# Warming matmuls back in front and all engine orders replaced, in a one-core linear attention with a squared-ReLU layer pair

## The chip, the cores and the metric

The kernel runs on one core of a Trainium2 chip. The metric is device microseconds of one execution. Five instruction streams work side by side and meet at semaphores: PE (matmuls), DVE (VectorE), ACT (ScalarE), POOL (GpSimd) and SP, which here only issues DMAs. POOL issues DMAs as well as computing.

## The reference

```python
# q, k, v, alpha: (4 batches, 8 heads, 768 tokens, 48), fp32
for t in range(S):
    state = alpha[:, :, t, :, None] * state + einsum('bhd,bhe->bhde', k[:, :, t], v[:, :, t])
    y[:, :, t] = einsum('bhd,bhde->bhe', q[:, :, t], state)
x = y.transpose(0, 2, 1, 3).reshape(3072, 384)
h = maximum(x @ w_in, 0)          # w_in (384, 2048)
out = (h * h) @ w_out             # w_out (2048, 384)
```

A recurrence over tokens with a decay per channel, then two dense layers with a squared ReLU between them.

## The kernel before

**Units.** The tokens are cut into 12 units of 256 tokens (three per batch, the batches taking turns). Each unit goes through a front (decays), scores, an output, a first dense layer and a second one. A number behind an underscore is the unit: `ln3` is the logarithm of unit 3.

**One unit.** Four loads bring alpha, k, q and v (`lda`, `ldk`, `ldq`, `ldv`) into RAW. ACT takes the Ln of alpha (`ln`), PE sums it over tokens with a triangular matrix (`m1`, `m1i`, `m1s`), ACT takes Exp of the sums with both signs (`ei`, `ea`, `es`) and of the total (`ec`). DVE multiplies k and q with them into QKS (`ekm`, `eqm`, lines 597, 731, 736). From unit 2 on, a product of the two alphas of a pair of tokens comes first (`pr`, lines 658 and 660) and `bk`, `aq` multiply one alpha back in (lines 687 to 698). QKS is transposed into KQT, for units 0 to 2 by PE with copies out (`tr`, `et`), from unit 3 on by two DMA transposes on SP (`tr0`, `tr1`, line 747). PE makes the scores (`p`, line 925) into two PSUM banks, DVE masks them (`mk`, line 936). `kv` makes the unit's own state, `sa`, `sc`, `sd` carry the state on, `y` is the attention output. It is copied (`xe`), transposed (`xt`; from unit 4 on by a DMA on SP) and, in the first units, copied once more (`xv`). `vc` casts v.

**The dense layers.** `s1_g_u` are eight blocks of six matmuls with 256 columns (line 1029); each ends in a relu out of PSUM (`re`, ACT line 1037 or DVE line 1039), and the relus are squared into GT (`sq`, DVE line 1047, POOL line 1050, ACT line 1051), two blocks at a time for the first six, one at a time for the last two. The relu's PSUM banks are mostly two halves used in turn. `s2_g_j_n` are blocks of four matmuls with 384 columns (line 1070) that read GT; `oe` copies their sum out, `out` stores it. The weights come in five pieces (`win0` to `win2`, `wout0`, `wout1`), loaded by POOL.

**What sets the order.** `ORDERS` holds, for every engine, the full list of its operations by name; which list a name stands in decides which engine does it, for those that have alternatives. `schedule()` walks these lists with a table of costs to get a planned start for each operation, and `place()` derives from the operations' reads and writes which semaphore waits are needed. No engine reorders anything: an operation that waits holds up all behind it in its list. Loads are gated besides (`AFTER`, `BEHIND`): win0 and the loads of k and alpha of unit 1 wait for alpha of unit 0 to land, win1 and q, v of unit 1 for k of unit 0, win2 for q of unit 0, unit 2's for win1, unit 3's for wout0, and each later unit's alpha for the q of the unit before.

**Warming matmuls.** `fill()` puts matmuls of ZERO by ZERO into the gaps of PE's planned start, from the landing of the memset of ZERO (an operation that is named `#19`) up to the first `s1_` block. In the lists of before, `#19` is DVE's last operation, behind everything else, so no such matmul is made.

**Named by number.** `#1` to `#13` and `#16` to `#18` are memsets on DVE; `#14`, `#15`, `#20` to `#22` are mask selects on POOL (`#21`, `#22` the two causal masks), `#23` is ACT's copy of half of a causal mask, `table` the load of ACT's function table.

The lines that place the warming matmuls:

```python
    pr.schedule()
    pr.fill(lambda n: lambda pe: pe.matmul(psO[:, 0:n], ZERO[:, 0:128], ZERO[:, 0:n], skip_group_check=True),
            ((512, 216, 420), (256, 109, 250)), min(o.start for o in pr.order["pe"] if o.name.startswith("s1_")), zero, 4600)
    pr.place()
```

and those of the load of a unit:

```python
            ring, cost, at = "sp", 600, L_PRIO[g] + j
            if name in QUEUE:
                ring, cost, at = "pool", 930, -6e5 + QUEUE.index(name)
            load_op[name] = add(ring, lambda e, dst=dst, src=src: e.dma_start(dst, src), cost, at,
                writes=[key], name=f"ld{name}", dma=f"{nm}{r}{ring}", lag=1230 if ring == "sp" else 1180, ...)
```

Of the kernel before, what the change touches and what calls it, by code (L numbers as in the profile page):

```python
# [3 lines left out]
ALU = mybir.AluOpType  # L4
# [9 lines left out]
        table ln0_0 ln1_0 ei0_0 #23 ei1_0 ea0_0 ec0_0 ea1_0 vc0 et01_0 ec1_0 ln1 ei1 ea1 xe0 et0_1 ec1 re0_2 re0_0  # L14
        re0_1 sq0_3 re0_5 re0_4 ln2 re0_6 re0_7 es2 ei2 sq0_7 re1_2 ea2 re1_3 sq0_6 re1_5 et1_2 re1_6 sq1_7 sq1_6
        sq1_5 ec2 sq1_1 ln3 oe0_0 ei3 ea3 ec3 es3 vc3 oe1_0 lm4 ln4 ei4 ea4 ec4 oe0_1 es4 re2_0 re2_1 oe1_1 re2_3
        sq2_3 re2_4 ln5 lm5 ei5 ea5 ec5 xe3 re2_7 re2_6 sq2_6 es5 re3_0 re3_1 oe2_0 vc5 re3_3 lm6 xe4 ln6 re3_4 ei6
        oe2_1 re3_7 ea6 ec6 es6 oe3_0 re4_1 re4_0 re4_3 ln7 xe5 ei7 ea7 lm7 ec7 es7 sq4_5 re4_6 re4_7 re5_0 re5_1
        sq4_7 sq4_6 re5_2 ln8 xe6 oe4_0 ei8 ea8 lm8 re5_5 re5_4 es8 sq5_5 re5_6 re5_7 re6_0 re6_1 sq5_6 ln9 re6_3 lm9
        re6_4 re6_5 ei9 ea9 es9 re6_7 re6_6 sq6_7 oe5_1 re7_1 re7_0 vc9 ln10 sq7_3 re7_5 ei10 lm10 ea10 re7_7 es10  # L20
        sq7_7 oe6_1 re8_1 sq7_5 re8_0 sq7_6 ln11 xe9 lm11 ei11 re8_4 oe7_0 re8_6 re8_5 sq8_6 ea11 re8_7 sq8_1 re9_0
        oe7_1 re9_2 es11 sq8_7 re9_4 oe8_0 xe10 sq9_1 re9_5 oe8_1 sq9_5 sq9_6 re10_1 oe9_0 oe9_1 re10_4 re10_5 re10_6
        re10_7 oe10_0 oe10_1 re11_4 sq11_5 re11_7 oe11_0 oe11_10
    """,
    "dve": """
        #7 #11 #4 #6 #5 #9 #10 #16 #12 #8 #13 #3 #1 #17 ekm0_0 ekm1_0 eqm0_0 #18 eqm1_0 et00_0 et10_0 et11_0 sa0 mk0_0
        mk1_0 ekm1 eqm1 xv0 et1_1 sc0 mk1_1 mk0_1 sa1 #2 re0_3 sq0_1 xe1 pr2 xv1 sq0_5 sc1 re1_0 re1_1 bk2 ekm2 eqm2
        re1_4 et0_2 re1_7 mk1_2 mk0_2 sa2 pr3 sc2 bk3 eqm1_3 ekm3 aq3 eqm0_3 pr4 xe2 sa3 xv2 lb4 ekm4 eqm1_4 eqm0_4
        sc3 re2_2 mk1_3 mk0_3 re2_5 sq2_5 sa4 ekm5 xv3 sc4 lb5 eqm1_5 eqm0_5 mk1_4 mk0_4 re3_2 sq3_3 sa5 re3_5 sc5
        sq3_5 bk6 ekm6 re3_6 lb6 eqm1_6 eqm0_6 mk1_5 mk0_5 re4_2 sq4_1 sa6 re4_4 re4_5 sc6 lb7 oe3_1 ekm7 eqm1_7  # L30
        eqm0_7 mk1_6 mk0_6 sd6 re5_3 sa7 sc7 sq5_3 lb8 ekm8 oe4_1 eqm1_8 eqm0_8 mk1_7 mk0_7 sq5_7 sq6_1 re6_2 xe7
# [25 lines left out]
        #22 #15 #21 #14 #20 lda1 ldk1 ldq1 win1 win0 ldv1 win2 lda2 ldq2 ldk2 ldv2 vc1 wout0 wout1 aq2 sq1_3 sd1 sd0
        vc2 sd2 bk4 sq2_1 pr5 vc4 sd3 bk5 sq2_7 sq3_1 sd4 pr6 sq3_7 sq3_6 vc6 sd5 pr7 sq4_3 bk7 vc7 pr8 sq5_1 bk8 vc8
        pr9 sq6_3 bk9 sq6_6 sq6_5 vc10 bk11 vc11 sq9_3 sq9_7 sq10_1 sq10_6 sq11_1 sq11_3
    """,  # L60
    "sp": """
        lda0 ldk0 ldq0 ldv0 lda3 ldq3 ldk3 ldv3 lda4 ldk4 ldv4 ldq4 tr0_3 tr1_3 lda5 ldk5 tr0_4 tr1_4 out0_1 ldq5 ldv5
        out1_1 lda6 tr0_5 ldk6 tr1_5 ldq6 xt4 ldv6 lda7 tr0_6 ldk7 tr1_6 ldq7 xt5 ldv7 out2_1 lda8 tr0_7 ldk8 tr1_7
        ldq8 xt6 ldv8 out3_1 lda9 tr0_8 ldk9 tr1_8 ldq9 xt7 ldv9 lda10 out4_1 tr0_9 tr1_9 ldk10 ldq10 ldv10 xt8 lda11
        out5_1 ldk11 out6_1 tr1_10 tr0_10 xt9 ldq11 ldv11 out7_1 tr0_11 tr1_11 xt10 out8_1 xt11 out9_1 out10_1 out11_0
        out11_10 out11_11
# [25 lines left out]
class Program:  # L92
# [65 lines left out]
    def schedule(self):  # L158
# [17 lines left out]
        shared = {"dve": 0.0, "pool": 0.0}  # L176
# [17 lines left out]
        while True:  # L194
# [167 lines left out]
def bass_gla_recurrent__then__act_relu_squared_kernel(  # L362
# [27 lines left out]
    RATIO = 4  # L390
    NRAW, NQKS, NKQT, NPM, NV, NXT, NGT, NRR, NOSB = 4, 3, 3, 2, 4, 4, 2, 4, 2
# [111 lines left out]
    def weight(name):  # L503
# [9 lines left out]
        load_op[name] = add("pool", lambda e: e.dma_start(dst, src), 930, -6e5 + QUEUE.index(name), writes=[(key, w)], name=name,  # L513
# [4 lines left out]
    def hd(ap):  # L518
        return ap.rearrange("p (h d) -> p h d", h=H)
# [9 lines left out]
    def load(g):  # L529
# [7 lines left out]
        for j, t, nm in ((0, alpha, "a"), (1, k, "k"), (2, q, "q"), (3, v, "v")):  # L537
# [5 lines left out]
            if name in QUEUE:  # L543
                ring, cost, at = "pool", 930, -6e5 + QUEUE.index(name)
            load_op[name] = add(ring, lambda e, dst=dst, src=src: e.dma_start(dst, src), cost, at,
                writes=[key], name=f"ld{name}", dma=f"{nm}{r}{ring}", lag=1230 if ring == "sp" else 1180,
# [106 lines left out]
    def decays_by_pair(g, p0, r, la, last):  # L653

        def al(j):
            return RAW[r][:, 0, :, j, :]
# [3 lines left out]
            alts={"pool": (lambda e: e.tensor_tensor(hd(PRD[la][:]), al(0), al(1), ALU.mult), pool_ns(HD))})  # L660
# [26 lines left out]
        add("pool", lambda e: e.tensor_tensor(hd(EK[la][:, 0, :]), hd(EK[la][:, 1, :]), al(1), ALU.mult), pool_ns(HD),  # L687
# [3 lines left out]
        if g < RATIO:  # L691
# [4 lines left out]
            add("pool", lambda e: e.tensor_tensor(hd(EQ[la][:, 0, :]), hd(EQ[la][:, 0, :]), al(0), ALU.mult), pool_ns(HD),  # L696
# [462 lines left out]
```

## Time and profile before

| | us |
|---|---|
| median of 3 runs | 176.27 |
| the runs | 173.71, 176.27, 177.86 |
| the profiled execution | 173.93 |
| its span, first to last instruction | 172.2 |
| PE busy / DVE / ACT / POOL | 160.9 / 117.2 / 104.5 / 64.6 |

The page of the profile gives the busy time of each engine, then the span in 40 slices with a digit for tenths of busy time, then the chain of work that ended last. The chain in order of time lists start, length, engine, tile and line of each piece. The timeline lists start, length, engine, line, operation, output and inputs, and in brackets the idle time before it with what ended it. Rows of grouped instructions end in busy time, mean nanoseconds of one, and idle time before them. A row of the table of stages begins with the stretch and its length, and gives busy time and count for each engine.

### The profile page before, as it was taken

How to read it: one execution, taken by the hardware profiler on the slowest of the kernel's cores; microseconds unless marked ns; L12 is line 12 of the kernel's file. 1: busy time of each engine (PE TensorE's matmuls, PEld its weight loads, DVE VectorE, ACT ScalarE, POOL GpSimd, SP SyncE). 2: the span in 40 equal slices, each digit the busy share in tenths (PEclk: the TensorE clock that was granted, in tenths of full speed). 3: DMA queues.
4: the chain of work that ended last, by engine and by line, in shares of the span. 5: the costliest groups of instructions: out<-in, count | busy, mean ns of one | idle time of the engine just before them, and what ended most of it. 6: DMA issues, size and time to landing. Idle time of an engine off the chain costs nothing.

```text
span 172.2 us, 5038 instructions
## 1 busy us (share of the span) xinstructions
PE 160.9 (93%) x2200; PEld 127.6 (74%) x2200; DVE 117.2 (68%) x186; ACT 104.5 (61%) x190; POOL 64.6 (37%) x65
## 2 busy tenths in 40 slices
PE   0696999999999999999999999999999999999994
PEld 0564799756788877887877887878777877687773
DVE  4478889768977787769566848799517709355241
ACT  2837478767677866466785578377668454152240
POOL 4947214910286554481640466001012122403700
PEclk9999999999999999999999999999999999999999
DMA  5999999999997999999999999999983672220012
GB/s 139 346 256 244 291 276 212 204 272 297 159 240 183 292 221 179 221 222 251 205 221 293 219 197 243 162 286 317 183 209 115 90 84 93 48 93 0 24 71 91
DMA packets 71559, 33.37 MB, mean 194 GB/s; under 512 B 67568, under 2 KB 68592, under 8 KB 71536
## 3 DMA queue, kind: packets, MB, share of 16 engines
q1 hardware_dynamic: 69024, 26.75, 70.4%
q0 software_dynamic: 2512, 6.29, 15.4%
q8 instruction: 17, 0.28, 0.7%
q14 instruction: 6, 0.05, 0.1%
HBM read 25.17 MB, written 4.72 MB: 174 GB/s over the span
## 4 chain that ended last, share of the span: by engine, by line
PE 90%; DVE 3%; ACT 2%; DMA 2%; issue 1%; DVEq 0%; ACTq 0%
PE psWH L1029 36%; PE psO L1070 33%; PE psX L925 3%; PE psZ L796 2%; PE psX L828 2%; DMA raw<-in_alpha_dram 2%; PE psX L817 2%; PE psWH L1070 2%; PE psX L997 2%; PE psZ L925 1%; PE psWH L669 1%; DVE pm L936 1%; PE psO L1029 1%; PE psX L864 1%; PE psX L971 1%
## 5 line engine op out<-in xcount | busy, mean ns | idle before, releaser
L1029 PE MATMUL psWH<-xt,win 128*128 128x256 bf16 x552 | 71.0, 274 | 0.2 <-ACT rr L1037 0.2
L1070 PE MATMUL psO<-wout,gt 128*128 128x384 bf16 x352 | 66.3, 326 | 0.0
L1029 PEld LDWEIGHTS psWH<-xt,win 128*128 128x128 bf16 x552 | 61.4, 129 | 5.3 <-DVE xt L983 0.6
L1070 PEld LDWEIGHTS psO<-wout,gt 128*128 128x128 bf16 x352 | 33.4, 98 | 17.5 <-DVE gt L1047 0.5
L1037 ACT ACTIVATE rr<-psWH 128x512 bf16<-128x512 f32 x58 | 33.9, 595 | 15.4 <-PE psWH L1029 14.5
L1050 POOL TENSOR_TENSOR gt<-rr 128x1024 bf16<-128x1024 bf16 (+1 forms) x17 | 28.0, 1654 | 37.4 <-ACT rr L1037 20.8
L1039 DVE TENSOR_SCALAR rr<-psWH 128x512 bf16<-128x512 f32 x34 | 23.4, 690 | 19.5 <-PE psWH L1029 19.0
L1051 ACT ACTIVATE gt<-rr 128x512 bf16<-128x512 bf16 (+1 forms) x26 | 21.1, 824 | 5.8 <-DVE rr L1039 5.8
L1077 ACT ACTIVATE osb<-psO 128x384 f32<-128x384 f32 x18 | 8.8, 490 | 17.0 <-PE psO L1070 16.8
L936 DVE TENSOR_TENSOR pm<-psZ,caus 128x1024 bf16<-128x1024 f32 x12 | 14.6, 1220 | 3.1 <-PE psZ L925 3.1
L726 POOL CAST vbf<-raw 128x768 bf16<-128x768 f32 x8 | 6.7, 832 | 24.6 <-DMA raw<-in_v_dram 24.6
L936 DVE TENSOR_TENSOR pm<-psX,caus 128x1024 bf16<-128x1024 f32 x12 | 14.6, 1216 | 0.5 <-PE psZ L925 0.5
L1047 DVE TENSOR_TENSOR gt<-rr 128x1024 bf16<-128x1024 bf16 (+1 forms) x17 | 10.6, 625 | 2.9 <-ACT rr L1037 2.4
L687 POOL TENSOR_TENSOR ek<-ek,raw 128x384 f32<-128x384 f32 x6 | 6.5, 1082 | 15.8 <-ACT ek L680 15.8
L731 DVE TENSOR_TENSOR qks<-raw,eq 128x384 bf16<-128x384 f32 x18 | 9.4, 553 | 2.6 <-DMA raw<-in_q_dram 1.8
L736 DVE TENSOR_TENSOR qks<-raw,ek 128x768 bf16<-128x768 f32 x11 | 10.5, 955 | 0.5 <-POOL ek L687 0.4
L704 DVE TENSOR_TENSOR la<-psWH,la 128x384 f32<-128x384 f32 x8 | 4.4, 553 | 7.9 <-ACT eq L682 6.5
L661 ACT ACTIVATE lab<-prd 128x384 bf16<-128x384 f32 x10 | 5.2, 522 | 4.1 <-POOL prd L660 2.4
L956 ACT ACTIVATE xbf<-psX 128x768 bf16<-128x768 f32 x7 | 5.7, 810 | 3.3 <-PE psX L817 3.0
L660 POOL TENSOR_TENSOR prd<-raw 128x384 f32<-128x384 f32 x5 | 5.2, 1040 | 4.9 <-DMA raw<-in_alpha_dram 4.9
L680 ACT ACTIVATE ek<-psWH 128x384 f32<-128x384 f32 x10 | 4.9, 490 | 3.0 <-PE psWH L672 2.2
L958 DVE CAST xbf<-psX 128x768 bf16<-128x768 f32 x5 | 4.8, 954 | 2.0 <-PE psX L817 1.3
(128 smaller groups left out, 183.7 us busy)
## 6 DMA issues: line engine op xcount, KB each, us to landing
out_dram<-osb SPq DMA_DIRECT2D x11, 384.0 KB, 4.0
raw<-in_alpha_dram SPq DMA_DIRECT2D x10, 384.0 KB, 4.5
raw<-in_k_dram SPq DMA_DIRECT2D x10, 384.0 KB, 4.6
raw<-in_q_dram SPq DMA_DIRECT2D x10, 384.0 KB, 4.8
raw<-in_v_dram SPq DMA_DIRECT2D x10, 384.0 KB, 4.9
wout<-in_moe_w_out_dram POOLq DMA_DIRECT2D x2, 768.0 KB, 8.4
raw<-in_alpha_dram POOLq DMA_DIRECT2D x2, 384.0 KB, 6.5
raw<-in_k_dram POOLq DMA_DIRECT2D x2, 384.0 KB, 7.2
```

What stands on the lines that cost most here:

```text
L731: add("dve", lambda e, j=j, dst=dst: e.tensor_tensor(dst, RAW[r][:, 2, :, j, :].rearrange("p (n x) d -> p n x d", x=2), EQ[la][:, j].rearr ...
L736: add("dve", lambda e, a=a, E=E: e.tensor_tensor(QKS[qs][:, a, :, :, 0:D], RAW[r][:, 1 + a].rearrange("p h j d -> p j h d"), E[la][:].rear ...
L925: ins = pe.matmul(psT[64 * c:64 * c + 64, rr_, o:o + 128], keys, mov)
L936: add("dve", lambda e, hf=hf, psT=psT: e.tensor_tensor(PM[pm][:, hf].rearrange("p r n j t -> p (r n) (j t)"), psT[:, :, :].rearrange("p r ...
L1029: ins = pe.matmul(psF[:, i * T:(i + 1) * T], WIN[:, kk, hidden(fj)], mov, start=(kk == 0), stop=(kk == KT - 1))
L1037: add("act", lambda e, psF=psF, rr=rr: e.activation(rr, psF, AF.Relu), act_ns(512), pu + 600, reads=[keyF], writes=[("rr", rb, half)], nam ...
L1039: alts={"dve": (lambda e, psF=psF, rr=rr: e.tensor_scalar(rr, psF, 0.0, None, ALU.max), dve_ns(512))})
L1047: add("dve", lambda e, dst=dst, sq=sq: e.tensor_tensor(dst, sq, sq, ALU.mult), 148 + k * 267, pu + 1200, reads=[("rr", rb, h) for h in ran ...
L1050: alts={"pool": (lambda e, dst=dst, sq=sq: e.tensor_tensor(dst, sq, sq, ALU.mult), 200 + k * 840), "act": (lambda e, dst=dst, sq=sq: e.act ...
L1051: "act": (lambda e, dst=dst, sq=sq: e.activation(dst, sq, AF.Square), act_ns(k * 512))})
L1070: ins = pe.matmul(psS, GT[gt][:, fj, j, :], WOUT[:, fj, :], start=(fj == 0), stop=(fj == FT - 1))
L1077: add("act", lambda e, j=j, psS=psS: e.activation(OSB[ob][:, j], psS, AF.Copy), act_ns(DM), ps_ + 700, reads=[keyS], writes=[("osb", ob, j ...
```

## The change

All five lists of `ORDERS` are new. 121 operations change their engine: 36 from DVE to ACT, 34 from ACT to DVE, 18 from POOL to DVE, 14 from ACT to POOL, 12 from DVE to POOL and 7 from POOL to ACT among the computing ones, beside one load. On PE the same blocks stand in another order. The planner's costs change, which act on the placing of the warming matmuls and on the lists that are written out, not on what an operation does. Loads of units 1 to 3 may stand in SP's or POOL's list; the lists put alpha of unit 1 (`lda1`) on SP and leave the others where they were.

The beginnings of the lists, and the stretches of PE's list around the scores of unit 6 and of SP's around its transposes:

```diff
  "act":
-  table ln0_0 ln1_0 ei0_0 #23 ei1_0 ea0_0 ec0_0 ea1_0 vc0 et01_0 ec1_0 ln1 ei1 ea1 xe0 et0_1 ec1 re0_2 re0_0
+  table #23 ln0_0 ln1_0 ei0_0 ea0_0 ei1_0 ea1_0 ec0_0 ec1_0 et00_0 ln1 ei1 ea1 xe0 et0_1 xv0 ec1 re0_1 re0_0
  "dve":
-  #7 #11 #4 #6 #5 #9 #10 #16 #12 #8 #13 #3 #1 #17 ekm0_0 ekm1_0 eqm0_0 #18 eqm1_0 et00_0 et10_0 et11_0 sa0 mk0_0
-  mk1_0 ekm1 eqm1 xv0 et1_1 sc0 mk1_1 mk0_1 sa1 #2 re0_3 sq0_1 xe1 pr2 xv1 sq0_5 sc1
+  #19 #1 #16 #5 #10 #6 #13 #2 #8 #17 #9 #11 #7 #12 #3 ekm0_0 #18 eqm0_0 ekm1_0 eqm1_0 et10_0 et01_0 et11_0 sa0
+  mk0_0 mk1_0 ekm1 eqm1 sc0 et1_1 mk1_1 mk0_1 sa1 #4 sc1 re0_2 sd1 pr2 xv1
   ...
-  oe11_11 #19
+  oe11_11
  "pe":
-  s1_4_5 s2_3_1_2 s2_3_1_3 s1_4_7 p0_6 s1_4_6 s2_4_0_0
+  s1_4_4 s2_3_1_2 s1_4_5 p0_6 s2_3_1_3 s1_4_7 s1_4_6 s2_4_0_0
  "pool":
-  #22 #15 #21 #14 #20 lda1 ldk1 ldq1 win1 win0 ldv1 win2 lda2 ldq2 ldk2 ldv2 vc1 wout0 wout1 aq2 sq1_3
+  #22 #21 #15 #14 #20 ldk1 ldq1 ldv1 win1 vc0 win0 win2 lda2 ldk2 vc1 ldq2 ldv2 wout0 sq0_3 wout1 vc2
  "sp":
-  lda0 ldk0 ldq0 ldv0 lda3 ... ldv6 lda7 tr0_6 ldk7 tr1_6 ldq7 xt5 ldv7 out2_1 lda8 tr0_7 ldk8 tr1_7
+  lda0 ldk0 ldq0 ldv0 lda1 lda3 ... ldv6 lda7 tr0_6 tr1_6 ldk7 ldq7 ldv7 xt5 out2_1 lda8 ldk8 tr0_7 tr1_7
```

The planner and the operations:

```diff
-    SBUF_ONLY = ("pr", "bk", "aq", "ekm", "eqm", "sq", "sb", "sd")
-    SWITCH = 95
+    ENTER = {"F": 11, "C": 195, "R": 195, "T": 220}
+    COLD = 9000
 ...
                 if e == "pe":
+                    if now < self.COLD:
+                        o.end += 0.6 * o.cost
                     if o.mode[0] != mode:
-                        o.end += self.SWITCH
+                        o.end += 57 if o.name.startswith("s1_") else self.ENTER[o.mode[0]]
                     mode = o.mode[1]
-                if e == "pool" and o.sem is None or e == "dve" and o.name.startswith(self.SBUF_ONLY):
-                    other = shared["dve" if e == "pool" else "pool"]
-                    o.end += max(0.0, min(other - now, 1200.0)) * (0.8 if e == "dve" else 0.5)
-                    shared[e] = o.end
 ...
+    EITHER = (1, 2, 3)
 ...
-        load_op[name] = add("pool", lambda e: e.dma_start(dst, src), 930, ...
+        load_op[name] = add("pool", lambda e: e.dma_start(dst, src), 760 if key == "win" else 650, ...
 ...
-            load_op[name] = add(ring, lambda e, dst=dst, src=src: e.dma_start(dst, src), cost, at,
-                writes=[key], name=f"ld{name}", dma=f"{nm}{r}{ring}", lag=1230 if ring == "sp" else 1180,
+            go = lambda e, dst=dst, src=src: e.dma_start(dst, src)
+            load_op[name] = add(ring, go, cost, at,
+                writes=[key], name=f"ld{name}", dma=f"{nm}{r}", lag=1230 if ring == "sp" else 1180,
+                alts={"sp": (go, 600), "pool": (go, 930)} if g in EITHER else None,
 ...
# pr, bk and aq, where they are on POOL:
-            ... pool_ns(HD)
+            ... pool_ns(HD) + 170
```

More of the change, by code (lines that the diff above doesn't have):

```diff
@@ L19 @@
[L19 to L23, printed above, removed]
+        table #23 ln0_0 ln1_0 ei0_0 ea0_0 ei1_0 ea1_0 ec0_0 ec1_0 et00_0 ln1 ei1 ea1 xe0 et0_1 xv0 ec1 re0_1 re0_0
@@ L27 @@
[L27 to L31, printed above, removed]
@@ L55 @@
+        s2_9_0_3 s1_10_2 s1_10_1 s2_9_1_0 y11 s2_9_1_1 s2_9_1_2 s2_9_1_3 s1_10_3 s1_10_4 s2_10_0_0 s1_10_5 s1_10_6
+        s2_10_0_1 s1_10_7 s2_10_0_2 s1_11_0 s2_10_0_3 s1_11_1 s1_11_2 s2_10_1_0 s2_10_1_1 s1_11_3 s2_10_1_2 s2_10_1_3
+        s1_11_4 s1_11_5 s2_11_0_0 s1_11_6 s1_11_7 s2_11_0_1 s2_11_0_2 s2_11_0_3 s2_11_1_0 s2_11_1_1
     """,
     "pool": """
-        #22 #15 #21 #14 #20 lda1 ldk1 ldq1 win1 win0 ldv1 win2 lda2 ldq2 ldk2 ldv2 vc1 wout0 wout1 aq2 sq1_3 sd1 sd0
-        vc2 sd2 bk4 sq2_1 pr5 vc4 sd3 bk5 sq2_7 sq3_1 sd4 pr6 sq3_7 sq3_6 vc6 sd5 pr7 sq4_3 bk7 vc7 pr8 sq5_1 bk8 vc8
@@ L59 @@
-        pr9 sq6_3 bk9 sq6_6 sq6_5 vc10 bk11 vc11 sq9_3 sq9_7 sq10_1 sq10_6 sq11_1 sq11_3
+        #22 #21 #15 #14 #20 ldk1 ldq1 ldv1 win1 vc0 win0 win2 lda2 ldk2 vc1 ldq2 ldv2 wout0 sq0_3 wout1 vc2 sq0_5 sd0
+        sq1_1 bk3 vc3 bk4 pr5 sq2_5 sq2_7 sq2_6 pr6 sq3_1 sd5 sq3_5 sq3_6 vc6 sq4_1 vc7 sq5_3 sq5_5 sd6 sq6_1 sq6_3
+        sq6_5 sq6_7 pr10 sq7_3 sq7_7 sq7_6 sq8_1 sq8_3 sd7 sq8_7 vc11 sq9_1 sq9_3 sq9_5 sq9_7 sq11_3 sq11_6
     """,
     "sp": """
-        lda0 ldk0 ldq0 ldv0 lda3 ldq3 ldk3 ldv3 lda4 ldk4 ldv4 ldq4 tr0_3 tr1_3 lda5 ldk5 tr0_4 tr1_4 out0_1 ldq5 ldv5
@@ L512, in weight @@
             dst = WOUT[:, w0:w0 + n, :].rearrange("p (s e) n -> p s (e n)", e=e)
-        load_op[name] = add("pool", lambda e: e.dma_start(dst, src), 930, -6e5 + QUEUE.index(name), writes=[(key, w)], name=name,
+        load_op[name] = add("pool", lambda e: e.dma_start(dst, src), 760 if key == "win" else 650, -6e5 + QUEUE.index(name), writes=[(key, w)], name=name,
                             dma=name, lag=8600 * n / 16, after=gate(name))
@@ L686, in decays_by_pair @@
                 reads=[("ps", "W")], writes=[("acm", la)], name=f"ec{g}")
-        add("pool", lambda e: e.tensor_tensor(hd(EK[la][:, 0, :]), hd(EK[la][:, 1, :]), al(1), ALU.mult), pool_ns(HD),
+        add("pool", lambda e: e.tensor_tensor(hd(EK[la][:, 0, :]), hd(EK[la][:, 1, :]), al(1), ALU.mult), pool_ns(HD) + 170,
             p0 + 700, reads=[("ek", la, 1), ("raw", r, 0)], writes=[("ek", la, 0)], name=f"bk{g}",
@@ L695, in decays_by_pair @@
                 reads=[keyM], writes=[("eq", la, 0)], name=f"es{g}")
-            add("pool", lambda e: e.tensor_tensor(hd(EQ[la][:, 0, :]), hd(EQ[la][:, 0, :]), al(0), ALU.mult), pool_ns(HD),
+            add("pool", lambda e: e.tensor_tensor(hd(EQ[la][:, 0, :]), hd(EQ[la][:, 0, :]), al(0), ALU.mult), pool_ns(HD) + 170,
                 p0 + 800, reads=[("eq", la, 0), ("raw", r, 0)], writes=[("eq", la, 0)], name=f"aq{g}",
```

72 lines of the change are left out of this document (39 added, 33 removed).

## The prediction

> **What bounds the kernel now.** I read the head of the page first: busy times, the 40 slices, the chain by engine.
>
> ```profile
> span 172.2 us, 5038 instructions
> ...
> PE 160.9 (93%) x2200; PEld 127.6 (74%) x2200; DVE 117.2 (68%) x186; ACT 104.5 (61%) x190; POOL 64.6 (37%) x65
> ...
> PE   0696999999999999999999999999999999999994
> ...
> DMA  5999999999997999999999999999983672220012
> ...
> PE 90%; DVE 3%; ACT 2%; DMA 2%; issue 1%; DVEq 0%; ACTq 0%
> ```
>
> PE is on 90% of the chain that ended last, and it is idle only in the first four slices and the last. The table of stages puts this in microseconds; I cut it where the chain first enters PE, where PE stops being fed by fits and starts, and where its last matmul ends.
>
> ```profile
> 0.00:4.93 4.93, 0.00 (x1) 0.01 (x1) 2.10 (x14) 1.86 (x3) 2.11 (x10) 1.00 0.63 163
> 4.93:17.61 12.68, 9.15 (x154) 7.00 (x154) 9.20 (x16) 8.06 (x16) 9.17 (x11) 1.00 1.14 278
> 17.61:169.90 152.29, 151.79 (x2046) 120.64 (x2046) 105.35 (x155) 94.60 (x172) 53.28 (x45) 1.00 0.86 189
> 169.90:172.20 2.30, 0.00 (x0) 0.00 (x0) 0.55 (x2) 0.00 (x0) 0.00 (x0) 1.00 0.26 86
> ```
>
> The columns after the length are PE, weight loads, DVE, ACT, POOL. From 17.61 to 169.90 PE is busy 151.79 of 152.29 us, so no order can gain more than some tenths there; it can only lose. What can be earned lies before 17.61 us, and in the price of changing from one kind of matmul to another. The front is a chain through all engines:
>
> ```profile
> 0.81 3.45 DMA raw<-in_alpha_dram
> 4.35 0.53 ACT laf L561
> ...
> 5.27 0.16 PE psX L568
> 5.43 0.16 PE psX L569
> ...
> 6.36 0.30 ACT caus L485
> ...
> 9.26 1.03 PE psZ L609 x8
> ...
> 12.81 1.23 DVE pm L936
> ...
> 14.99 0.82 ACT xbf L956
> ...
> 16.40 0.56 DVE xt L983
> 16.96 0.61 DVE kqt L766
> ...
> 18.25 0.78 PE psO L1029 x6
> ```
>
> The first alpha lands at 4.26; the first dense matmul of the first layer starts just before 18.25. In it PE runs at half rate: eight 128x128 transposes took 1.03 us at 9.26, and the same eight took 0.62 us at 14.99 in the timeline:
>
> ```profile
> 14.99 0.62 PE L759 MATMUL psZ<-ident,qks 128*128 128x128 bf16 x8
> ```
>
> **Part 1: Zeros first, hence warming matmuls.** In the program before, the memset of ZERO is DVE's last instruction, and fill places its dummy matmuls only after it, so there are none. Now it is DVE's first, and the built order shows 25 matmuls of 512 columns and 5 of 256 in the gaps of PE's front: nine and two ahead of the first real one, the rest between the stages up to the second scores. Cost: L568 to L569 is 0.16 us for 192 columns, 0.83 ns a column, so 512 columns cold take 0.43 us and the first eleven 9 x 0.43 + 2 x 0.21 = 4.3 us. ZERO is ready after one memset:
>
> ```profile
> 0.93 0.27 DVE L456 MEMSET qks<- 128x256 uint32 x1 [0.93 <-PEq L1144]
> ...
> 2.67 0.42 POOL L459 TENSOR_SCALAR_AFFINE_SELECT caus<-caus 128x256 bf16<-128x256 bf16 x1 [2.16 <-DVE caus L456]
> ...
> 6.26 0.40 ACT L485 ACTIVATE caus<-caus 64x256 bf16<-64x256 bf16 x1
> ```
>
> They start near 1.3 and end near 5.6 if cold throughout, where the first real matmul could start at about 5.05: up to 0.55 us lost, nothing if the clock has risen before. What a warm clock gives: the cold PE pieces of the front chain are 0.9 (decays, from 4.93 to 5.85), 1.03 (transposes), 0.76 (state) and 0.60 (scores), 3.3 us in all; at 0.62 for 1.03 they shrink by 40%, 1.3 us. The upper bound of the gain is that; the lower is none, if the warm clock comes no sooner.
>
> The Trainium skill (TensorE: Matmul & The Clock Gate, "Part 1: The HAM clock gate") says the clock opens after a busy window of about 3.4 us that runs freely. By it the fills open the gate somewhere between 4.7 and 8.1 us, and the sum would keep between a half and all of that gain. The transposes above agree with two rates; when the gate opens after fills no run here shows.
>
> **Part 2: the rest of the front.** The caus1 memset goes back from ninth to fourteenth on DVE (end about 3.2 instead of 2.6), both mask selects on POOL follow it, and ACT's copy of the mask (0.40 us) now stands ahead of the first Ln: Ln starts some 0.15 late, but the copy no longer parts the two Exp of the chain (0.30 us at 6.36): 0.15 saved. The cast of v to VBF leaves ACT for POOL, where it waits for v ahead of the issue of win0 and win2. The copy of XT leaves DVE for ACT: of the 0.56 at 16.40, which stood ahead of the 0.61 that released the second scores, most is saved. On ACT it starts after a 1.02 us copy of KQT and ends near 16.7, no later than the other operand. Its floor is the weight load:
>
> ```profile
> win<-in_moe_w_in_dram POOLq DMA_DIRECT2D x2, 384.0 KB, 7.0
> ```
>
> POOL now issues win0 behind the v load and the cast, near 9.1, so it lands at 16 to 17.8; PE's first block now needs win0. Freedom of queue is used once: alpha of unit 1 moves to SP, behind v of unit 0, issued at the landing of alpha 0 as before. SP's other calls wait for wout0 (30 us), so nothing is queued behind it. The 1.3 of the warm clock, 0.15 and 0.3 to 0.5 from XT add to 1.8; less up to 0.55 of fill overrun, and cut by the landing of win0 to about 17.4 against 18.2: I take -0.8 us, ends -1.5 and +0.3.
>
> **Part 3: changes of kind on PE.** The same blocks run in another order. Counted in the two lists, scores, outputs and states are followed by a first-layer block 13 times before and 4 times after, by a second-layer block 10 and 19 times.
>
> ```profile
> 69.48 0.76 PE psO L1070 x4
> ...
> 71.55 0.65 PE psO L1070 x4
> ...
> 78.28 0.66 PE psWH L1029 x6
> 78.93 0.16 issue
> 79.09 0.42 PE psX L925 x16
> ...
> 79.73 0.81 PE psWH L1029 x6
> ```
>
> Right after scores a second-layer block costs 0.11 more than elsewhere (0.76, 0.65), a first-layer block 0.15 (0.81, 0.66). Nine times 0.04 is -0.4 us, ends -0.6 and 0.
>
> **Part 4: attention asked for earlier.** Unit 6's scores (79.09 above) now stand two blocks earlier, 1.3 us, and with the front's gain PE asks for them near 76.7. They need two transposes through SP:
>
> ```profile
> 70.17 2.22 SPq L747 DMA_TRANSPOSE kqt<-qks  x1
> 72.44 0.58 SPq L545 DMA_DIRECT2D raw<-in_k_dram  x1
> 73.06 1.33 SPq L747 DMA_TRANSPOSE kqt<-qks  x1
> ...
> DMA to landing us min/median/max: 5.8/5.8/5.8
> ```
>
> The second landed at 78.9. The SP list now puts both transposes ahead of that load, so the second is issued at 72.4 and with 4 to 5.8 us lands at 76.4 to 78.2. Wait: 0 to 1.5, I take +0.2. Scores of units 8 and 10 stand five blocks (3.3 us) earlier, those of 9 and 11 later; each of these two can pay the same.
>
> **Part 5: DVE against POOL.** POOL takes 8 more double squares of the hidden layer and 3 more single ones, and gives up four products of 1.08, two of 1.04, and some casts and smaller products. The kernel's planner no longer charges DVE and POOL for overlapping; POOL's products get a flat 170 ns. The rows speak for a real conflict:
>
> ```profile
> 29.33 0.95 DVE L736 TENSOR_TENSOR qks<-raw,eq 128x768 bf16<-128x768 f32 x1
> ...
> 29.47 2.57 POOL L1050 TENSOR_TENSOR gt<-rr 128x1024 bf16<-128x1024 bf16 x1 [1.88 <-ACT rr L1037]
> ...
> 161.50 1.90 POOL L1050 TENSOR_TENSOR gt<-rr 128x1024 bf16<-128x1024 bf16 x1 [0.72 <-DVE rr L1039]
> ...
> L1039 DVE TENSOR_SCALAR rr<-psWH 128x512 bf16<-128x512 f32 x34 | 23.4, 690 | 19.5 <-PE psWH L1029 19.0
> ...
> L731 DVE TENSOR_TENSOR qks<-raw,eq 128x384 bf16<-128x384 f32 x18 | 9.4, 553 | 2.6 <-DMA raw<-in_q_dram 1.8
> ```
>
> A POOL square that takes 1.90 alone took 2.57 when it started 0.14 after a DVE product of 0.95: longer by 0.67, about the rest of that product. And in the timeline, of DVE's instructions after 13 us, the 60 with both inputs in SBUF (the products at L731 and the like) never start inside a POOL instruction, of the 99 others (the relus at L1039 and the like) 41 do. Either they waited, or the old order kept them apart. The new one does not aim to: 73 such DVE instructions (64 before), and POOL busy about 53.3 + 15.9 + 3.1 less some 11 for what it gives up, 61 of 152 us, 40%. Some 28 of them would meet POOL, each for 0.75 us on average (half a POOL instruction, weighted by length): 21 us of waiting on DVE, which has 172 - 117 = 55 us idle. How much reaches PE? The relus waited 19.0 us for PE in 18 of 34 cases, so half of them had about 1 us in hand and half nothing. I take one meeting in four as reaching PE, with 0.75 less half a block (0.33), 0.42 us: 7 x 0.42 = +2.9 us. Ends: 0, where the meetings fall into DVE's idle time, and +7, where every second one reaches PE with 0.5.
>
> The Trainium skill (SBUF — State Buffer, "Who interferes with whom") says that a VectorE instruction with two SBUF inputs and a GpSimd one that reads SBUF exclude each other, and that the second to issue blocks for the whole of the first. The 2.57 us agree for POOL as the one that waits; DVE as the one that waits no run here shows. By the rule the sum is the one above; without it, it is that sum less 2.9.
>
> **The sum.** The profiled execution took 173.93 us, 1.73 more than its span, which stays. 173.93 - 0.8 - 0.4 + 0.2 + 2.9 = 175.8 us. The runs shown lie at 173.71, 176.27 and 177.86, so the profiled one is near the fastest and 2.3 below the median; I add nothing for that, since the fills take away one cause of spread that I can see, a cold PE whose clock rises at one time or another. Against the median, 175.8 is -0.3%. About 2% is what a measurement of this kernel tells from no change: below 172.7 or above 179.8.
>
> **The rivals.**
> A, kept apart (0.26): the new order hides the meetings as well as the old. Speaks for it: DVE idles 55 us, POOL 108; against: nothing in the planner asks for it now. 173.93 - 0.8 - 0.4 - 0.5 (the half microsecond of PE idle after 17.61) = 172.2, faster by 2.3%.
> B, DVE behind POOL's squares (0.24): at the relus of the first layer, whose PSUM halves PE wants back after a block or two. Half of 28 meetings reach PE: 173.93 - 1.2 + 0.2 + 7 = 179.9, slower. It decides against the median from 3.5 us of PE waits on, and to over 2% from 7. For it: squares of 1.9 on POOL where 8 were shorter on ACT or DVE; against: half of the relus have time in hand.
> C, SP late and the meetings hidden (0.07): units 6, 8 and 10 wait 1.5 us each at their scores: 173.93 - 1.2 + 4.5 = 177.2, no change. For it: the 5.8 us row; against: both transposes now go first.
> D, the fills warm nothing (0.07): the gate opens no sooner than before and they only push the first matmul by 0.55: 175.8 + 0.8 + 0.3 = 176.9, no change.
>
> **How the numbers follow.** The forecast has 0.36. Faster: A, 0.26. Within 2%: forecast, C and D, 0.50. Slower: B, 0.24. The range takes in A and B to their prices, 172.0 to 180.0; beyond stand the better half of A and the worse half of B, two in ten.
>
> **What would show it.** Fills: PE busy from about 1.3 us, the eight transposes of unit 0 near 0.6, the first L1029 block near 17.4; wrong if it stands past 18. Meetings: DVE products with idle time that ends with a POOL square, POOL squares well over 1.9, and PE waits on relus or on GT after 17.61; if PE there is again busy to half a microsecond, part 5 is wrong and A right. Part 4: an idle PE ahead of L925 near 77.

## The result, and the profile after

The changed kernel takes 184.56 us (median of 4: 183.15 to 185.75), the one before on the same chip 175.25 (173.71 to 177.86): 1.056 times as long, 95% interval 1.042 to 1.070. The comparisons leave disturbed executions out, so a ratio below can differ from that of two medians, most of all for the old kernel with warming matmuls, where six of twelve are left out. The forecast of 175.8 and its range up to 180.0 missed it. The head of the page after:

```profile
span 182.6 us, 5111 instructions
...
PE 167.3 (92%) x2230; PEld 128.2 (70%) x2230; DVE 134.1 (73%) x190; ACT 100.7 (55%) x185; POOL 75.7 (41%) x65
...
PE   7879987699999779999999799899996999999994
...
PE 36%; DVE 21%; DMA 16%; ACT 7%; issue 2%; SPq 1%; DVEq 0%
```

The profiled execution took 184.31. PE now starts at once, but in eight of the slices after the fourth and before the last it falls below nine tenths, where before there was none, and DVE has 21% of the chain that ended last instead of 3%, DMAs 16% instead of 2%. The table of stages, cut at the same places as in the prediction (first real matmul, scores of unit 1, last matmul):

```profile
0.00:5.25 5.25, 4.00 (x11) 1.54 (x12) 2.39 (x15) 2.43 (x4) 2.18 (x10) 1.00 0.66 174
5.25:17.48 12.23, 10.57 (x175) 6.58 (x173) 9.97 (x15) 7.62 (x15) 8.23 (x11) 1.00 1.15 279
17.48:180.10 162.62, 152.60 (x2046) 120.07 (x2046) 121.43 (x159) 90.67 (x167) 65.33 (x46) 1.00 0.85 177
180.10:182.60 2.50, 0.13 (x3) 0.00 (x0) 0.28 (x1) 0.00 (x0) 0.00 (x0) 0.98 0.24 79
```

The third row holds nearly all of it: the same 2046 matmuls took 162.62 us instead of 152.29. PE is idle there 10.02 us instead of 0.50 and busy 0.81 longer; ahead of it 0.13 was gained, behind it 0.20 lost. That is the span's 10.4. In the same stage DVE's busy time rose by 16.1 us (105.35 before), although it has only four instructions more. The costliest groups say which:

```profile
L1039 DVE TENSOR_SCALAR rr<-psWH 128x512 bf16<-128x512 f32 x28 | 19.1, 686 | 8.5 <-PE psWH L1029 8.3
...
L731 DVE TENSOR_TENSOR qks<-raw,eq 128x384 bf16<-128x384 f32 x18 | 13.6, 789 | 3.9 <-DMA raw<-in_q_dram 2.8
...
L736 DVE TENSOR_TENSOR qks<-raw,ek 128x768 bf16<-128x768 f32 x11 | 12.2, 1110 | 0.3 <-DMA raw<-in_k_dram 0.2
L689 DVE TENSOR_TENSOR ek<-ek,raw 128x384 f32<-128x384 f32 x8 | 9.5, 1193 | 3.8 <-ACT ek L680 3.7
...
L658 DVE TENSOR_TENSOR prd<-raw 128x384 f32<-128x384 f32 x7 | 6.6, 948 | 2.1 <-DMA raw<-in_alpha_dram 2.1
```

The relus and the masks, which read one operand from PSUM, take what they took (686 and 1217 ns, 690 and 1220 before). The products with both operands in SBUF are drawn out: L731 from 553 to 789 ns, L736 from 955 to 1110, L689 from 556 to 1193, L658 from 550 to 948. The row of L689 before:

```profile
L689 DVE TENSOR_TENSOR ek<-ek,raw 128x384 f32<-128x384 f32 x4 | 2.2, 556 | 1.4 <-ACT ek L680 1.3
```

Twenty-two of the 69 such products after 13 us start inside a POOL instruction, and 21 of them are drawn out. Before, one of 60 did (at 107.65, in the last 0.05 us of a square), at its usual length. The worst stretch in the timeline, DVE, POOL and PE:

```profile
22.56 2.25 DVE L658 TENSOR_TENSOR prd<-raw 128x384 f32<-128x384 f32 x1
...
27.22 1.82 DVE L689 TENSOR_TENSOR ek<-ek,raw 128x384 f32<-128x384 f32 x1
28.97 1.19 DVE L698 TENSOR_TENSOR eq<-eq,raw 128x384 f32<-128x384 f32 x1
30.25 2.48 DVE L736 TENSOR_TENSOR qks<-raw,eq 128x768 bf16<-128x768 f32 x1
32.65 0.94 DVE L736 TENSOR_TENSOR qks<-raw,ek 128x768 bf16<-128x768 f32 x1
```

```profile
22.27 2.13 POOL L1050 TENSOR_TENSOR gt<-rr 128x1024 bf16<-128x1024 bf16 x1 [0.73 <-DVE rr L1039]
...
26.74 1.89 POOL L1050 TENSOR_TENSOR gt<-rr 128x1024 bf16<-128x1024 bf16 x1
28.60 1.14 POOL L900 TENSOR_TENSOR sbd<-tmp,acm 128x384 bf16<-128x384 f32 x1
29.70 2.21 POOL L1050 TENSOR_TENSOR gt<-rr 128x1024 bf16<-128x1024 bf16 x1
```

```profile
33.65 1.07 PE L759 MATMUL psZ<-ident,qks 128*128 128x128 bf16 x16 [3.02 <-DVE qks L736]
```

POOL's square of 22.27 runs to 24.40; the DVE product of 22.56, 0.55 us alone, stands to 24.81, 0.41 past the square. The square of 26.74 ends at 28.63, the product of 27.22 at 29.04, again 0.41 later; the square of 29.70 ends at 31.91, the product of 30.25 (0.96 alone) at 32.73, 0.82 later. Each of the three ends 0.14 us short of its own length after the POOL instruction in which it began. A blocked product has no idle time ahead of it in the trace; its own row becomes longer. PE, whose block before ended at 30.62, had the transposes of unit 2 at 33.65.

### The profile page after: what moved, and what is told of

Same layout as the page of the kernel before. It is cut to its first block, busy times and chain, and to the rows that moved or that the text cites. A ratio compares the mean times of both kernels' runs of the same rounds, so it can differ in the third digit from the quotient of the medians.

```text
span 182.6 us, 5111 instructions
## 1 busy us (share of the span) xinstructions
PE 167.3 (92%) x2230; PEld 128.2 (70%) x2230; DVE 134.1 (73%) x190; ACT 100.7 (55%) x185; POOL 75.7 (41%) x65
## 4 chain that ended last, share of the span: by engine, by line
PE 36%; DVE 21%; DMA 16%; ACT 7%; issue 2%; SPq 1%; DVEq 0%
PE psO L1070 16%; PE psWH L1029 12%; DMA raw<-in_q_dram 5%; DVE qks L736 4%; DVE pm L936 4%; DVE qks L731 4%; DMA kqt<-qks 4%; DMA xt<-xbf 4%; DMA raw<-in_alpha_dram 3%; DVE rr L1039 2%; PE psX L997 1%; DVE ek L689 1%; DVE gt L1047 1%; ACT ek L680 1%; DVE prd L658 1%
## 5 line engine op out<-in xcount | busy, mean ns | idle before, releaser
L1029 PE MATMUL psWH<-xt,win 128*128 128x256 bf16 x552 | 70.5, 273 | 3.6 <-DMA xt<-xbf 1.7
L1050 POOL TENSOR_TENSOR gt<-rr 128x1024 bf16<-128x1024 bf16 (+1 forms) x28 | 48.8, 1747 | 56.2 <-ACT rr L1037 30.4
L1029 PEld LDWEIGHTS psWH<-xt,win 128*128 128x128 bf16 x552 | 61.5, 129 | 9.8 <-ACT rr L1037 2.0
L1037 ACT ACTIVATE rr<-psWH 128x512 bf16<-128x512 f32 x64 | 37.2, 596 | 30.9 <-PE psWH L1029 30.1
L1039 DVE TENSOR_SCALAR rr<-psWH 128x512 bf16<-128x512 f32 x28 | 19.1, 686 | 8.5 <-PE psWH L1029 8.3
L936 DVE TENSOR_TENSOR pm<-psZ,caus 128x1024 bf16<-128x1024 f32 x12 | 14.6, 1217 | 3.9 <-PE psZ L925 3.9
L731 DVE TENSOR_TENSOR qks<-raw,eq 128x384 bf16<-128x384 f32 x18 | 13.6, 789 | 3.9 <-DMA raw<-in_q_dram 2.8
L1051 ACT ACTIVATE gt<-rr 128x512 bf16<-128x512 bf16 (+1 forms) x15 | 12.3, 827 | 0.2
L736 DVE TENSOR_TENSOR qks<-raw,ek 128x768 bf16<-128x768 f32 x11 | 12.2, 1110 | 0.3 <-DMA raw<-in_k_dram 0.2
L689 DVE TENSOR_TENSOR ek<-ek,raw 128x384 f32<-128x384 f32 x8 | 9.5, 1193 | 3.8 <-ACT ek L680 3.7
L1127 PE MATMUL psO<-zero 128*128 128x512 bf16 (+1 forms) x30 | 8.9, 434 | 1.3 <-DVE zero L454 1.3
L658 DVE TENSOR_TENSOR prd<-raw 128x384 f32<-128x384 f32 x7 | 6.6, 948 | 2.1 <-DMA raw<-in_alpha_dram 2.1
L687 POOL TENSOR_TENSOR ek<-ek,raw 128x384 f32<-128x384 f32 x2 | 2.0, 998 | 14.7 <-ACT ek L680 14.7
L660 POOL TENSOR_TENSOR prd<-raw 128x384 f32<-128x384 f32 x3 | 3.0, 1004 | 11.3 <-DMA raw<-in_alpha_dram 11.3
```

The source lines that it names most:

```text
L689: alts={"dve": (lambda e: e.tensor_tensor(hd(EK[la][:, 0, :]), hd(EK[la][:, 1, :]), al(1), ALU.mult), dve_ns(HD))})
L731: add("dve", lambda e, j=j, dst=dst: e.tensor_tensor(dst, RAW[r][:, 2, :, j, :].rearrange("p (n x) d -> p n x d", x=2), EQ[la][:, j].rearr ...
L736: add("dve", lambda e, a=a, E=E: e.tensor_tensor(QKS[qs][:, a, :, :, 0:D], RAW[r][:, 1 + a].rearrange("p h j d -> p j h d"), E[la][:].rear ...
L936: add("dve", lambda e, hf=hf, psT=psT: e.tensor_tensor(PM[pm][:, hf].rearrange("p r n j t -> p (r n) (j t)"), psT[:, :, :].rearrange("p r ...
L1029: ins = pe.matmul(psF[:, i * T:(i + 1) * T], WIN[:, kk, hidden(fj)], mov, start=(kk == 0), stop=(kk == KT - 1))
L1037: add("act", lambda e, psF=psF, rr=rr: e.activation(rr, psF, AF.Relu), act_ns(512), pu + 600, reads=[keyF], writes=[("rr", rb, half)], nam ...
```

## The experiments

**POOL's reads taken away.** The changed kernel with each of POOL's 44 computing instructions turned into two memsets of about the same length, which read nothing (line numbers are 4 higher; the squares stand for all):

```diff
-  e.tensor_tensor(dst, sq, sq, ALU.mult)
+  (e.memset(DUMO[:, 0:k * 512], 0.0), e.memset(dst, 1.0))[-1]
```

> The lists of after, unchanged; each of POOL's 44 computing instructions (squares, products, casts of v, state updates; not the mask selects) becomes two memsets, one of a scratch tile and one of the tile that it wrote, of about the length of before, so that POOL computes for as long but reads no SBUF. The squares, casts and products done on POOL are left out. Theory (exclusion of DVE's two-input products and POOL's reads): DVE busy falls from 134 to 117 to 119 us, no product is longer than alone, PE's waits after the first dense block fall from 12 us to 1 to 4, 174.5 to 178 us. Rival (the new order asks PE for attention before SP and the loads can serve it, or POOL is simply later than ACT or DVE would be): DVE busy falls too, PE's waits stay above 8 us, 181 us or more.

Measured: 176.47 us (10 runs), ratio to before 1.003 (0.998 to 1.009). DVE's groups, POOL's, and the stage:

```profile
L740 DVE TENSOR_TENSOR qks<-raw,ek 128x768 bf16<-128x768 f32 x11 | 10.5, 953 | 1.1 <-ACT ek L650 0.6 <-DMA raw<-in_k_dram 0.5
...
L735 DVE TENSOR_TENSOR qks<-raw,eq 128x384 bf16<-128x384 f32 x18 | 9.4, 554 | 8.2 <-DMA raw<-in_q_dram 6.3 <-ACT eq L686 0.9 <-ACT gt L1055 0.9
L693 DVE TENSOR_TENSOR ek<-ek,raw 128x384 f32<-128x384 f32 x8 | 4.5, 556 | 3.9 <-ACT ek L684 3.8
...
L662 DVE TENSOR_TENSOR prd<-raw 128x384 f32<-128x384 f32 x7 | 3.9, 554 | 3.4 <-DMA raw<-in_alpha_dram 3.4
```

```profile
L1054 POOL MEMSET dumo<- 128x1024 f32 (+1 forms) x28 | 23.0, 820 | 55.6 <-ACT rr L1041 29.3 <-DVE rr L1043 25.5
L1054 POOL MEMSET gt<- 128x1024 bf16 (+1 forms) x28 | 22.7, 812 | 0.0
```

```profile
17.93:172.10 154.17, 151.82 (x2046) 120.25 (x2046) 105.14 (x159) 90.14 (x167) 60.18 (x89) 1.00 0.88 187
```

With the same orders (each of POOL's instructions depends besides on the one ahead of it in its list) and a POOL busy 1.63 us for each square (1.75 with the squares themselves), every product is back at its length, DVE is busy 116.9 us, and 7.7 of the 10.0 us of PE's idle time are gone. What else the change does cannot be told from nothing: at most 0.9%. The forecast for this theory, 174.5 to 178, holds. The Trainium skill (SBUF — State Buffer, "Who interferes with whom") says that a VectorE instruction with two SBUF inputs contends with a GpSimd one that reads SBUF, and not with one that only writes it. These rows agree with both halves of it, and the rows of the result show DVE as the one that waits.

**Three squares moved to ACT.** In the changed kernel the squares of 22.27, 26.74 and 29.70 (`sq0_3`, `sq0_5`, `sq1_1`) leave POOL's list for ACT's (here and in the next two, line numbers are 11 lower):

```diff
  "act":  ... sq0_1 re0_3 +sq0_3 xe1 re0_4 ln2 re0_6 es2 +sq0_5 ei2 ... re1_3 +sq1_1 sq0_7
  "pool": ... wout0 -sq0_3 wout1 vc2 -sq0_5 sd0 -sq1_1 bk3
```

> The lists of after, with only the first three squares of POOL (sq0_3, sq0_5, sq1_1) moved to ACT. Theory: the four DVE products of unit 2's front that took 2.25, 1.82, 1.19 and 2.48 us take 0.55, 0.55, 0.55 and 0.95, and PE's two waits of 0.9 and 3.2 us before 34 us shrink to less than 1 in all: 3 us off after, 180.5 to 182.5 us. Rival (unit 2's front is late because its loads or PE's early asking set it): those waits keep 3 us or more, 183.5 us or more.

Measured: 180.91 us (179.77 to 182.36), ratio 1.033 (1.024 to 1.043). The same stretch:

```profile
22.86 0.55 DVE L647 TENSOR_TENSOR prd<-raw 128x384 f32<-128x384 f32 x1
...
27.72 0.56 DVE L678 TENSOR_TENSOR ek<-ek,raw 128x384 f32<-128x384 f32 x1 [0.69 <-ACT ek L669]
28.20 0.55 DVE L687 TENSOR_TENSOR eq<-eq,raw 128x384 f32<-128x384 f32 x1
28.84 0.96 DVE L725 TENSOR_TENSOR qks<-raw,eq 128x768 bf16<-128x768 f32 x1
```

```profile
30.72 1.07 PE L748 MATMUL psZ<-ident,qks 128*128 128x128 bf16 x16
```

PE's transposes start at 30.72 instead of 33.65, and PE's waits before 34 us fall from 3.75 to 0.41 us, as the theory had it. Three instructions out of 65 on POOL were worth 3.7 us of the median.

**All squares that met a product, and all squares, moved to ACT.** The same edit for the 15 double or single squares beside which a product was drawn out, and for all 28:

> The lists of after, with only those 15 of POOL's squares moved to ACT that overlap a lengthened DVE product in the profile of after. Theory: DVE busy 119 to 125 us, PE's waits 2 to 6 us, 175 to 179 us; the meetings shift, so some new ones. Rival: 182 us or more.

> The lists of after, with all 28 squares of POOL moved to ACT, each put where ACT stood when POOL began it in the profile of after. ACT gets 26 us more on 101, POOL keeps products, casts and state updates. Theory: few meetings are left, DVE busy 118 to 123 us, PE's waits 3 to 7 us (some new ones, since relus now stand behind squares on ACT), 176 to 180 us. Rival (order or SP): 182 us or more.

Measured: 179.32 us for the fifteen, ratio 1.021 (1.015 to 1.028), DVE busy 120.2; 180.13 for all, ratio 1.024 (1.015 to 1.033), DVE busy 122.3, ACT 121.4. Both times lie just above their ranges. Most of the meetings are gone: six and nine products are still drawn out, by 3.3 and 5.3 us in all, against 21 by 17.8 in the changed kernel. Of what is left, much ends with ACT: with the fifteen moved, seven of PE's twelve waits after the first block do, 3.0 of 3.9 us. The waits of PE's weight loads in that kernel (us in total, times, longest):

```profile
PEld psX L960 <- ACT xbf L945: 1.6, 3, 0.6
...
PEld psWH L1018 <- ACT rr L1026: 1.5, 2, 1.2
...
PEld psO L1059 <- ACT osb L1066: 1.1, 2, 0.8
```

So moving the squares trades one wait for another. The old lists left 17 of them on POOL, placed so that only one product of DVE began inside one, at its very end.

**The fills alone.** In the kernel before, ZERO's memset first instead of last on DVE, which brings the warming matmuls back and changes nothing else; and the reverse in the changed kernel:

```diff
  "dve":
-  #7 #11 #4 ... oe11_11 #19
+  #19 #7 #11 #4 ... oe11_11
```

> The lists of before, with one edit: the memset of ZERO goes from the last to the first place on DVE, so the warming matmuls are made. Theory (DVE products and POOL instructions that read SBUF shut each other out, and only the new lists make them meet): PE's waits after the first dense block stay near the 1.1 us of before, DVE's busy time near 117 us, the clock rises near 5 us instead of 12.2, the first dense block starts 0.3 to 0.9 us earlier than 18.19, and the time is 173.0 to 173.9 us. Rival (the warming matmuls themselves disturb): 175 us or more.

> The lists of after, with the memset of ZERO put back to DVE's last place: no warming matmuls. Theory: PE's waits of 12.0 us and DVE's 134 us busy stay, the cold front costs 0.3 to 1.3 us, so 184.5 to 185.8 us. Rival (the warming matmuls are what costs): 176 us or less.

Measured: the kernel before with fills 177.82 (12 runs), ratio 1.003 (0.997 to 1.008); the changed kernel without them 184.66, inside its range, ratio to before 1.047 (1.039 to 1.055). They neither bring a gain that can be measured nor cause the loss. For the old kernel the 173.0 to 173.9 was missed; it had been set from the fastest execution, and the kernel before had a median of 175.78 on that chip. In the execution of it that was profiled (178.70 us) five products are drawn out beside POOL's instructions, by 4.8 us in all: the old lists keep them apart in the execution that was profiled before, but not in every one.

In the changed kernel the clock is granted at 4.99 us with them and at 11.63 without, and yet the first block of L1029 starts later with them, at 18.05 against 17.56. DVE's four products of unit 0 end with these rows, with fills and, second, without:

```profile
8.02 1.60 DVE L597 TENSOR_TENSOR qks<-raw,eq 128x384 bf16<-128x384 f32 x1
```

```profile
8.03 0.55 DVE L597 TENSOR_TENSOR qks<-raw,eq 128x384 bf16<-128x384 f32 x1
```

With fills the last one met POOL's cast of v, which the change had put there (0.84 us from 8.36), and stood 1.05 longer; DVE's first mask of unit 0 starts 0.42 later (11.38 against 10.96). Without fills the starts are nearly the same, but there the product kept its length and the cast (from 8.31) took 0.96. The starts do not settle which of the two had to wait.

This meeting is not all that ate the warm clock's gain. In the kernels with memsets and with three squares moved the product is at its length, and yet the first block of the first layer stands at 18.51 and 18.35. There the fills themselves are in the way. In the kernel with memsets:

```profile
13.05 1.35 PE L1131 MATMUL psO<-zero 128*128 128x512 bf16 x6
14.33 0.36 PE L861 MATMUL psX<-smd,kqt 128*64 128x96 bf16 x8
```

The masks of unit 0 were done at 13.26, and its output stood behind six fills until 14.33; with three squares moved they were done at 12.62, and the output started at 14.17. `fill()` puts them into the gaps of the planned starts, and PE takes its list in order whether the gap is there or not.

**Reads against writes in the kernel before.** Eleven instructions of 1.8 to 1.9 us were added to POOL's old list, ten of them ahead of a `sd`, `bk` or `pr`: products that read SBUF in one kernel, memsets in the other. Both kernels also set the scratch tile once, ahead of POOL's first loads.

```diff
+  add("pool", lambda e: e.tensor_tensor(DUMO[:, 0:1024], DUMI[:], DUMI[:], ALU.mult), 1900, ...)   # the one
+  add("pool", lambda e: e.memset(DUMO[:], 0.0), 1900, ...)                                         # the other
```

> The lists of before, with eleven extra POOL instructions on a scratch tile that nothing waits for, each a product of two SBUF inputs of 1024 bf16 (some 1.9 us, 21 us in all), behind eleven of POOL's own. Theory: DVE's products become longer where they meet them, DVE busy 4 to 9 us above 117, PE waits 2 to 6 us, 176 to 180 us. Rival (POOL's work is only late for those who wait for it): DVE busy stays at 117, and the time is that of the run with eleven writes.

> The same lists with the same eleven places, but each extra POOL instruction is a memset of 2048 fp32 of a scratch tile, which reads no SBUF (meant to last about 1.9 us too). Theory: DVE busy stays near 117 us and the time within 1 us of before, 173.5 to 175. Rival (POOL late): the same time as with eleven reads.

Measured: reads 183.9 us, ratio 1.042 (1.033 to 1.051), DVE busy 126.2; memsets 181.52, ratio 1.033 (1.027 to 1.039), DVE busy 120.2. Both ranges were missed (176 to 180, and 173.5 to 175): a POOL that is late costs much by itself. With memsets:

```profile
58.59 1.78 DVE L736 TENSOR_TENSOR qks<-raw,ek 128x768 bf16<-128x768 f32 x1 [3.29 <-POOL ek L687]
```

```profile
60.89 1.65 PE L1029 MATMUL psWH<-xt,win 128*128 128x256 bf16 x12 [2.91 <-DVE xt L983]
```

POOL's product of L687 stood behind two memsets, DVE waited 3.29 us for it, and the copy of XT behind that on DVE kept PE waiting for 2.91. With reads the same wait is 3.02. The span of the memset kernel is 7.4 us longer than before: 4.3 are waits of PE after the first block, which itself stands 1.1 later, with the clock granted at 17.74 instead of 12.24, and 3.41 us at half speed (last section) are left for most of the rest.

By their times, 0.9% apart with intervals that overlap, the two kernels would not settle the lock; their rows do. The same product beside an added read and, second, beside an added memset:

```profile
139.78 1.35 DVE L731 TENSOR_TENSOR qks<-raw,eq 128x384 bf16<-128x384 f32 x1
138.82 1.89 POOL L1128 TENSOR_TENSOR dumo<-dumi 128x1024 f32<-128x1024 bf16 x1
```

```profile
139.48 0.55 DVE L731 TENSOR_TENSOR qks<-raw,eq 128x384 bf16<-128x384 f32 x1
138.50 1.81 POOL L1128 MEMSET dumo<- 128x2048 f32 x1
```

Seven products begin inside an added read, and six of them are drawn out, by 0.50 to 1.60 us (the seventh began 0.18 before its end). Ten begin inside an added memset, and each keeps its length. The reads add 6.0 us to DVE's time; the 3.0 that the memsets add are three products beside POOL's own squares, which now stand later. In the changed kernel POOL's lateness is not what counts: with memsets of like length there, nothing that can be measured was lost.

**Towards a mend.** The changed kernel with the fifteen squares on ACT, no fills, and unit 0's cast of v back on ACT:

```diff
  "act":  table #23 ... ec0_0 ec1_0 +vc0 et00_0
  "dve":  -#19 #1 #16 ... oe11_11 +#19
  "pool": ... win1 -vc0 win0 win2
```

> The changed kernel with three edits: the 15 double squares that met a lengthened DVE product are on ACT (as in the run that moved those alone: 179.3 us, DVE busy 120.2, span 177.2), the memset of ZERO is last on DVE again (so no fills), and the cast of unit 0's v is on ACT again, behind the two copies of the mask block, so that the window's issue no longer waits for it on POOL and eqm1_0 meets no cast. Lock theory (meetings were the loss, the rest of the loss is now ACT being late): the front gains 0.5 to 1.0 (first L1018 block, a row of the first layer, near 17.1 to 17.6, against 18.06 with the change), nothing else moves: 178.3 to 178.9, still slower than before by 1.4 to 1.8%. If it comes to 176 or less, the front's price was larger than its place in the trace says, by delays that it hands on. Rival (the fills are worth their warm clock): without them 179.5 to 180.5.

Measured: 180.75 us (178.17 to 181.19), ratio 1.019 (1.008 to 1.031), above the 178.3 to 178.9 expected. It cannot be told from the fifteen squares alone. Its profile does not answer for the front: the clock fell to half from 17.07 to 23.90 there, and the first block of L1018 stands at 19.82. No version that I ran beats the kernel before.

## Why the prediction was wrong

**Part 5, the step that failed.** The mechanism was named, and its first half came out nearly as worked: 28 meetings of 0.75 us were forecast, 21 us of waiting; 22 were counted, and DVE's busy time rose from 117.2 to 134.1. With POOL's reads turned into memsets it is 116.9, so the meetings hold 17.2 us: 1.05 in the front and 0.73 for each of the 22. What failed is the share that reaches PE. The forecast let one meeting in four through with 0.42 us (2.9 us), and the upper end every second one with 0.5 (7 us). PE's idle time in the stage rose by 9.5 us, and 7.7 of these go when POOL's reads go. That is more than the upper end, and not because each meeting reached PE a little: PE waited at twelve places, the longest for 3.02 us behind a whole row of meetings.

Two premises carried the small share. The slack was read from the wrong instructions: that half of them "had about 1 us in hand" was read off the relus, which read PSUM and are not drawn out (676 to 693 ns each). Eighteen of the 22 products belong to the attention of a coming unit, for which PE's order has a fixed place. And the meetings were treated as single, each with half a block of slack to spend. In the stretch from 22 to 34 us they stand in a row on one chain (`pr2`, `bk2`, `aq2`, `eqm2`): 1.70, 1.26, 0.64 and 1.52 us over their lengths alone, 5.1 together, against which one slack stands; undoing them gave 3.7 us. The other waits were not taken apart one by one. The sign that was named, idle time of DVE that ends with a POOL square, did not show: the wait is inside the product's own row.

**Rival B** had the sign, a chance of 0.24 and 179.9 us. It put the damage at the relus of the first layer, which took 686 ns against 690, and its price was half of the meetings. Its point of decision, 3.5 us of PE waits, was passed nearly three times over. (What the prediction puts beyond its range, half of A and half of B, adds up to 0.25 and not to two in ten.)

**Rival A** fails: the new order does not keep the meetings apart. Of the two readings that the prediction left open, waiting or kept apart, the old rows decide for the second: a product that waits is drawn out, and none of the 60 was (the "never" was off by one, the product at 107.65). The old lists were made with a planner that charged for the overlap, and the new ones without; that the charge is what kept them apart is likely, but no run separates it from the rest of the planner.

**Part 1.** PE is busy from 1.25 us and the clock is granted at 4.99, inside the stated 4.7 to 8.1, so rival D's mechanism is false; the first real matmul stands 0.32 later (5.25 against 4.93), and four transposes of unit 0 take 0.40 us instead of 0.61. But the first L1029 block stands at 18.05, past the 18 that was named as wrong: the gain of 1.3 did not come. In the old kernel fills brought the first block from 18.19 to 17.97. The term counted what the fills cost only ahead of the first real matmul, not those in the later gaps.

**Part 2.** The front without fills gained 0.63 us (17.56 against 18.19), as worked out for these edits (0.45 to 0.65); with them 0.14, with the product drawn out beside the cast of v on POOL, which had been costed as waiting only for v, and with the fills' own price. The term was -0.8.

**Part 3** forecast 0.4 us less on PE for the changes of kind. The same 2046 matmuls were busy 0.81 us longer in the stage. Ends of matmuls ahead of a wait are modelled, so that figure is not proof of a loss. With POOL's reads turned into memsets, the same order of blocks and 2.35 us of idle time they are busy 151.82, against 151.79 before: no gain.

**Part 4** forecast 0.2 us of waiting ahead of unit 6's scores. There is none, though PE came to them at 83.98 and not near 76.7 (77.0 by the prediction's own terms):

```profile
83.23 0.82 PE L1029 MATMUL psWH<-xt,win 128*128 128x256 bf16 x6
83.98 0.42 PE L925 MATMUL psX<-kqt 64*64 64x128 bf16 x16
```

Nor does PE wait at the scores of any later unit, with the meetings or, in the kernel with memsets, without them. Rival C falls with it. PE did wait for transposes through SP at two places, for XT of the layer (0.32 us to 88.96 and 1.41 to 140.30); whether these have a cause of their own beside the meetings stays open, but in the run with memsets one such wait of 0.84 us remains.

## What to carry to other kernels

When a change drops a term from a planner's cost, look first at what the old order shows that this term may have bought: 1 of 60 products began inside a POOL instruction with the charge, and 22 of 69 without it. Count slack at the instructions that are delayed, not at others of the same engine, and add up delays along one chain before any slack is taken off. In this kernel, work on POOL that reads SBUF is free for DVE only while DVE has no product of two SBUF operands; giving it to ACT instead moved the wait. Warming matmuls in planned gaps cost time here where a gap closed.

## What the runs showed of the hardware

After a long wait PE's clock can fall back in the middle of the kernel. Three stretches of the kernel with added products, in a table of stages that shows PE alone (after the stretch: length, PE busy, clock, DMA share, GB/s):

```profile
53.37:56.78 3.41, 2.20 (x53) 1.00 1.00 203
56.78:60.20 3.42, 1.05 (x10) 1.00 1.08 314
60.20:63.61 3.41, 2.76 (x16) 0.50 0.58 145
```

The kernel with added memsets has the same a little later: PE busy for 1.20 us from 58.68 to 62.09, then half speed until 65.50. In the changed kernel without warming matmuls a wait of 3.64 us, ending at 33.77, left the clock alone:

```profile
28.70:32.11 3.41, 1.42 (x14) 1.00 1.00 219
32.11:35.53 3.42, 1.76 (x24) 1.00 0.89 231
```

In the front of the mend it fell after a busier stretch:

```profile
13.66:17.07 3.41, 2.03 (x56) 1.00 1.20 210
17.07:20.48 3.41, 2.53 (x44) 0.50 1.10 270
```

The stretches are steps of 3.41 us from the moment at which the clock was granted in each run (12.41, 17.74, 11.63 and 13.66 us), and the falls lie on such steps. The Trainium skill (TensorE: Matmul & The Clock Gate, "Part 1: The HAM clock gate") gives a free-running window of 3413 ns, with which these lengths agree, and lets the clock fall after an idle window; the windows before these falls were not idle, but busy for 1.05, 1.20 and 2.03 of 3.41 us. After one of 1.42 full speed stayed, so PE's busy share of the window before does not decide it by itself, and what does is not shown here. One such step at half speed costs up to 1.7 us of work (an estimate: half of 3.41).
